# Dummy matmuls in TensorE's waits of the first batch, three first tiles beside their bank, and both q scalings of a half ahead

## The chip, the core and the metric

The kernel runs on one core of one Trainium2 chip. The core has five engines with a queue each, which run side by side and wait for each other through semaphores: TensorE (PE; its weight loads are shown as PEld), VectorE (DVE), ScalarE (ACT), GpSimd (POOL) and SyncE (SP). Each engine works through its own queue in order. The metric is the device time of one execution in microseconds; lower is better.

## What is computed

An attention layer with a cosine reweighting feeds a mixture of experts. Batch 8, 8 heads, 576 positions, head size 64; 8 experts with 512 -> 1024 -> 512.

```python
def phi(x, c, s):                       # c, s: cos and sin of a position's angle
    r = np.maximum(x, 0.0)
    return np.concatenate([r * c, r * s], axis=-1)
q_p, k_p = phi(q, cos_w, sin_w), phi(k, cos_w, sin_w)
kv = np.einsum('bhsf,bhsd->bhfd', k_p, v)
z = np.sum(k_p, axis=2)
num = np.einsum('bhsf,bhfd->bhsd', q_p, kv)
den = np.einsum('bhsf,bhf->bhs', q_p, z)[..., None] + 1e-06
x = num / den                           # heads side by side: 4608 x 512
...
P = balanced(exp(x @ w_gate))           # eight rounds over rows and columns
for e in range(E):
    out += P[:, e:e + 1] * (np.maximum(x @ w1[e], 0.0) @ w2[e])
```

## The kernel before

**Stages.** The first stage does the attention, batch after batch, and puts the first expert's two matmuls (ffn1, ffn2) between the attention's steps. The later stages balance P and run the other seven experts. The change lies in the first stage alone: in the first batch (lines 588 to 622), which has no expert work to lie between, in block j = 0, which holds the second batch's attention, and in block j = 1.

**The attention of one batch.** It goes in two halves of two head pairs (hk 0, 1 and 2, 3):
- `prep_q` scales q by cos and sin on VectorE (tile q_p). In batches 0 and 1 `turn` then transposes it on TensorE, three chunks a matmul bank, three banks a head pair, and ScalarE or VectorE takes each bank out with the relu (q_pT). From batch 2 on a transposing DMA on SP's queue does it.
- `prep_k` (relu, on ScalarE or VectorE), `prep_kp` (scaling on VectorE, tile k_p), `prep_v` (a copy into v_aug).
- `begin` is 36 small matmuls, k_p with v_aug. `made` takes the results out: zsel on VectorE, kv_sb on ScalarE.
- `denominators` is TensorE's q_pT with zsel, then VectorE's reciprocal and its split into a high and a low part (den, hi, hl).
- `attend` spreads hl over the rows (three matmuls; ScalarE copies the result to rb), multiplies q_pT with kv_sb, and VectorE multiplies both into xT, the input of the experts.

**The first expert's first tiles.** `first(kt)` adds the share of head pair kt to the first four tiles of ffn1 (two banks h_ps, two banks y_ps), each 128x512; after kt = 3 ScalarE takes them out (hT). Block 0 then begins with slot 4: slots 4 to 7 are ffn1's tiles, 8 to 15 ffn2's halves. `at(block, slot, fn, ...)` hangs a step of the attention behind a slot.

**Dummies.** `keep_busy(n)` (line 239) issues n matmuls of ones, 128x128x128, into a bank that nobody reads. Before the change there are 80 at the start and 14 ahead of the first half's sums. Their bank is one of the two of y_ps; the fourth of `first`'s tiles takes it over.

**What sets the order.** On TensorE, VectorE and ScalarE instructions are issued in the order in which the program is written (class `InOrder`, lines 101 to 118). The pools' buffers set waits on top of it: four banks small_ps, two h_ps, two y_ps, three buffers q_p, four k_p, four of each load. The loads stand in GpSimd's queue, written at lines 215 to 237 and in `load`: q, k and v of the first batch, the first expert's w1 in four parts, k, v and q of the second batch, w2 in two parts, then the batches that follow.

## Time and profile before

| | us |
|---|---|
| median of 7 runs | 996.55 |
| lowest and highest | 992.6 and 997.46 |
| the profiled execution's own time | 992.84 |
| its span, first to last instruction | 991.1 |
| TensorE busy in the span | 969.7 (98%) |
| VectorE, ScalarE, GpSimd busy | 809.1, 568.2, 59.0 |
| mean granted clock of TensorE in the span | 0.995 |

The profile is of one execution; its times count from the first instruction. A busy time is the sum of the instructions' durations on an engine. A line of the order of time has start, duration, engine, line, operation, output <- inputs, shape and count; what stands in brackets at its end is the idle time just before and the tile or DMA that ended it. Most instructions are issued through a helper and have its line, 109, so tiles tell them apart. A row of the busy table by stretches has the stretch, its length, the busy time and the count of instructions of PE, PEld, DVE, ACT and POOL, then the granted clock (1.00 is full), the busy share of the DMA engines (over 1 with overlapping packets) and GB/s.

### The profile page before, as it was taken

How to read it: one execution, taken by the hardware profiler on the slowest of the kernel's cores; microseconds unless marked ns; L12 is line 12 of the kernel's file. 1: busy time of each engine (PE TensorE's matmuls, PEld its weight loads, DVE VectorE, ACT ScalarE, POOL GpSimd, SP SyncE). 2: the span in 40 equal slices, each digit the busy share in tenths (PEclk: the TensorE clock that was granted, in tenths of full speed). 3: DMA queues.
4: the chain of work that ended last, by engine and by line, in shares of the span. 5: the costliest groups of instructions: out<-in, count | busy, mean ns of one | idle time of the engine just before them, and what ended most of it. 6: DMA issues, size and time to landing. Idle time of an engine off the chain costs nothing.

```text
span 991.1 us, 20149 instructions
## 1 busy us (share of the span) xinstructions
PE 969.7 (98%) x7804; PEld 674.7 (68%) x7804; DVE 809.1 (82%) x1840; ACT 568.2 (57%) x1267; POOL 59.0 (6%) x80
## 2 busy tenths in 40 slices
PE   7899999989999999999999999999999999999997
PEld 5445544447777777777777777777777777777775
DVE  6677675679889878988889888988789888988887
ACT  5576665457776555555555555555555555555551
POOL 6203110010000000000000000000000000000001
PEclk8999999999999999999999999999999999999999
DMA  9949991623013320043113410133103400104535
GB/s 163 207 87 155 158 151 32 133 45 90 25 49 67 62 54 25 25 92 67 34 40 67 82 34 26 41 76 67 49 25 68 91 25 25 49 25 111 132 86 128
DMA packets 80304, 73.54 MB, mean 74 GB/s; under 512 B 33232, under 2 KB 72144, under 8 KB 80208
## 3 DMA queue, kind: packets, MB, share of 16 engines
q0 software_dynamic: 27200, 30.94, 19.8%
q1 hardware_dynamic: 52768, 41.06, 16.9%
q8 instruction: 61, 1.00, 0.4%
q14 instruction: 35, 0.29, 0.1%
q10 hardware_dynamic: 240, 0.26, 0.1%
HBM read 83.12 MB, written 12.98 MB: 97 GB/s over the span
## 4 chain that ended last, share of the span: by engine, by line
PE 92%; DVE 3%; ACT 2%; DMA 1%; POOL 1%; issue 0%; POOLq 0%; ACTq 0%; SPq 0%
PE rows_ps L109 34%; PE h_ps L109 28%; PE copied_ps L109 11%; PE p_ps L109 11%; PE y_ps L109 5%; PE small_ps L109 4%; DMA v_ld<-in_v_dram 1%; ACT acc_lo L109 1%; DMA q_pT<-q_p 0%; DVE den L109 0%; DVE acc_hi L887 0%; POOL hs_last L902 0%; DVE P_tok L109 0%; DMA out_dram<-acc_lo 0%; DVE colp L109 0%
## 5 line engine op out<-in xcount | busy, mean ns | idle before, releaser
L887 DVE SCALAR_TENSOR_TENSOR acc_lo<-rows_ps,P_tok,acc_lo 128x512 f32<-128x512 f32 (+1 forms) x322 | 203.1, 639 | 74.4 <-PE rows_ps L109 74.3
L109 PEld LDWEIGHTS <-H 128*128 128x128 f16 x2080 | 203.0, 98 | 83.1 <-issue 1.2
L823 ACT CAST u<-h_ps 128x384 f16<-128x384 f32 x288 | 137.8, 478 | 131.1 <-PE h_ps L109 131.1
L109 PEld LDWEIGHTS <-w1e 128*128 128x128 f16 x1632 | 157.0, 98 | 68.4 <-issue 8.8
L817 DVE CUSTOM_DVE_ANT_0 H<-p_ps,u 128x384 f16<-128x384 f32 x329 | 180.8, 550 | 6.6 <-PE p_ps L109 6.4
L109 PEld LDWEIGHTS <-hs 128*128 128x128 f16 x1500 | 146.6, 98 | 56.2
L109 PE MATMUL h_ps<-S,w1e 128*128 128x384 f16 x672 | 164.1, 326 | 1.1 <-ACT u L109 0.9
L109 PE MATMUL p_ps<-xT,T 128*128 128x384 f16 x672 | 164.1, 326 | 0.1
L109 PE MATMUL h_ps<-xT,w1e 128*128 128x384 f16 (+1 forms) x616 | 151.5, 353 | 0.3 <-DVE xT L109 0.3
L109 PE MATMUL rows_ps<-V,H 128*128 128x256 f16 x1000 | 150.0, 273 | 0.7 <-DVE acc_hi L887 0.7
L109 PE MATMUL rows_ps<-w2e,hs 128*128 128x256 f16 x1000 | 150.0, 273 | 0.0
L855 ACT ACTIVATE H<-h_ps 128x384 f16<-128x384 f32 x144 | 70.7, 491 | 95.0 <-PE h_ps L109 95.0
L109 PEld LDWEIGHTS <-T 128*128 128x128 f16 x1008 | 98.1, 98 | 29.5 <-issue 3.1
L109 PE MATMUL rows_ps<-w2e,H 128*128 128x256 f16 (+1 forms) x568 | 91.2, 285 | 0.0
L836 ACT COPY copied_ps<-h_ps 128x384 f32<-128x384 f32 x144 | 67.5, 468 | 35.4 <-PE h_ps L109 35.4
L846 ACT ACTIVATE H<-copied_ps 128x384 f16<-128x384 f32 x144 | 70.9, 492 | 20.3 <-PE copied_ps L109 20.3
L109 PE MATMUL h_ps<-S,T 128*128 128x384 f16 x336 | 81.8, 325 | 0.4 <-ACT copied_ps L109 0.3
L109 PE MATMUL copied_ps<-xT,w1e 128*128 128x384 f16 x336 | 82.1, 326 | 0.0
L109 PE MATMUL copied_ps<-w2e,H 128*128 128x256 f16 x504 | 75.6, 272 | 0.0
L109 PE MATMUL rows_ps<-V,hs 128*128 128x256 f16 x500 | 75.0, 272 | 0.0
L887 DVE SCALAR_TENSOR_TENSOR acc_lo<-copied_ps,P_tok,acc_lo 128x256 f32<-128x256 f32 x126 | 60.0, 476 | 0.6 <-PE copied_ps L109 0.2
L887 DVE SCALAR_TENSOR_TENSOR acc_hi<-rows_ps,P_tok,acc_hi 128x512 f32<-128x512 f32 (+1 forms) x56 | 41.2, 736 | 20.5 <-PE rows_ps L109 19.7
(144 smaller groups left out, 952.2 us busy)
## 6 DMA issues: line engine op xcount, KB each, us to landing
S<-x_saved SPq DMA_DIRECT2D x108, 192.0 KB, 2.4
out_dram<-acc_lo SPq DMA_DIRECT2D x62, 128.0 KB, 2.4
w1e<-in_moe_w_dram POOLq DMA_DIRECT2D x7, 1024.0 KB, 9.1
w2e<-in_moe_w_dram POOLq DMA_DIRECT2D x7, 1024.0 KB, 10.1
q_ld<-in_q_dram POOLq DMA_DIRECT2D x16, 288.0 KB, 7.5
k_ld<-in_k_dram POOLq DMA_DIRECT2D x16, 288.0 KB, 8.6
v_ld<-in_v_dram POOLq DMA_DIRECT2D x16, 288.0 KB, 9.2
x_saved<-S SPq DMA_DIRECT2D x18, 192.0 KB, 1.9
```

The costliest lines, as they stand in the source:

```text
L109: i = getattr(self.engine, name)(*args, **kwargs)
L817: latest = ve._custom_dve(TENSOR_ADD_SAT, out=out, in0=ps[:, 0:TU], in1=t[:], s0=FP32_MAX, s1=0.0)
L823: se.copy(out=t[:], in_=ps[:, 0:TU])
L836: se.copy(out=Y[:, 0:TU], in_=X[:, 0:TU])
L846: se.activation(out=h11, in_=Y[:, 0:TU], func=AF.Relu)
L855: se.activation(out=h12, in_=X[:, 0:TU], func=AF.Relu)
L887: ve.scalar_tensor_tensor(out=a, in0=rows, scalar=P_tok[:, g, self.e : self.e + 1], in1=a, op0=ALU.mult, op1=ALU.add,)
```

## The change

The first batch's order is written anew, and dummies are put between its steps:
- `turn_all` and `attend` get a parameter `busy`: so many dummies after each turn, or between attend's two matmul groups.
- The dummies keep their bank; `first` has three tiles, and block 0 begins with slot 3. The steps that hung at slots 4 to 7 move a slot ahead or behind (begin(1, 0) is now behind slot 4), and k, v of the second batch's first half are prepared ahead of first(3).
- Both q scalings of a half are issued ahead: q of hk 2 ahead of `made`, q of hk 3 ahead of the denominators, and the turns of hk 3 ahead of attend(0, 0).
- The second v copy of each half goes to VectorE. The denominators of the second half stand ahead of first(1), first(2) between the two attends.
- In block 1 (j = 1) sums, denominators and attends hang one slot later, q of hk 2 is scaled in block 0, k of hk 1 in block 1.

```diff
--- before.py
+++ after.py
@@ -489,7 +489,7 @@
             for h in heads:
                 hls[b, h // 2] = hl
 
-        def attend(b, hk):
+        def attend(b, hk, busy=0):
 
             parts = ((0, 2 * C3), (2 * C3, C))
             rb_ps = [ps_s.tile([P, 512], FP32, name="small_ps") for _ in parts]
@@ -504,6 +504,7 @@
                         stop=True,
                     )
                 se.copy(out=rb[:, c0 * HP : c1 * HP], in_=rb_ps[i][:, 0 : (c1 - c0) * HP])
+            keep_busy(busy)
             num_ps = [ps_s.tile([P, 512], FP32, name="small_ps") for _ in parts]
             for i, (c0, c1) in enumerate(parts):
                 for hh in range(2):
@@ -560,7 +561,7 @@
                 first_ps.extend(
                     ps_h[0].tile([P, TCH], FP32, name="h_ps") if i < 2
                     else ps_y.tile([P, Dm], FP32, name="y_ps")
-                    for i in range(4)
+                    for i in range(3)
                 )
             for ft, h_ps in enumerate(first_ps):
                 te.matmul(
@@ -573,9 +574,10 @@
                 if kt == KT - 1:
                     se.activation(out=hT[:, ft, 0:TCH], in_=h_ps[:], func=AF.Relu)
 
-        def turn_all(b, hk, scalar=None):
+        def turn_all(b, hk, scalar=None, busy=0):
             for i in range(3):
                 turn(b, hk, i, scalar)
+                keep_busy(busy)
 
         begun = {}
 
@@ -587,57 +589,64 @@
 
         for hk in (0, 1):
             prep_q(0, hk)
-            turn_all(0, hk, True)
+            turn_all(0, hk, True, 4)
         for hk in (0, 1):
             prep_k(0, hk, False)
             prep_kp(0, hk)
-        keep_busy(14)
-        for hk in (0, 1):
-            prep_v(0, hk, se.copy)
+        keep_busy(8)
+        prep_v(0, 0, se.copy)
+        prep_v(0, 1, ve.tensor_copy)
         begin(0, 0)
         epsilons(0)
+        prep_q(0, 2)
         made(0, 0)
-        prep_q(0, 2)
+        prep_q(0, 3)
+        keep_busy(4)
         denominators(0, range(4))
-        turn_all(0, 2, True)
+        turn_all(0, 2, True, 4)
         prep_k(0, 2)
-        prep_q(0, 3)
-        attend(0, 0)
+        turn_all(0, 3, True, 4)
+        keep_busy(10)
+        prep_kp(0, 2)
+        attend(0, 0, 8)
         prep_k(0, 3)
+        prep_kp(0, 3)
         prep_v(0, 2, se.copy)
-        prep_kp(0, 2)
-        turn_all(0, 3)
-        prep_v(0, 3, se.copy)
-        attend(0, 1)
-        prep_kp(0, 3)
+        prep_v(0, 3, ve.tensor_copy)
+        attend(0, 1, 4)
         first(0)
         begin(0, 1)
         epsilons(0)
         made(0, 1)
+        keep_busy(4)
+        denominators(0, range(4, 8))
         first(1)
-        denominators(0, range(4, 8))
-        attend(0, 2)
-        attend(0, 3)
+        keep_busy(24)
+        attend(0, 2, 8)
         first(2)
+        attend(0, 3, 6)
+        for hk in (0, 1):
+            prep_k(1, hk, False)
+            prep_kp(1, hk)
+            prep_v(1, hk, se.copy)
         first(3)
 
         for j in range(B):
             b = j + 1
             if j == 0:
 
-                for half in range(2):
-                    for hk in (2 * half, 2 * half + 1):
-                        at(0, 4 + half, prep_k, 1, hk, False)
-                        at(0, 4 + half, prep_kp, 1, hk)
-                        at(0, 4 + half, prep_v, 1, hk, se.copy)
-                at(0, 5, begin, 1, 0)
-                at(0, 5, made, 1, 0)
-                at(0, 6, prep_q, 1, 0)
-                at(0, 6, prep_q, 1, 1)
-                at(0, 7, begin, 1, 1)
-                at(0, 7, turn_all, 1, 0)
-                at(0, 7, made, 1, 1)
-                at(0, 7, prep_q, 1, 2)
+                at(0, 4, begin, 1, 0)
+                at(0, 4, made, 1, 0)
+                for hk in (2, 3):
+                    at(0, 4, prep_k, 1, hk, False)
+                    at(0, 4, prep_kp, 1, hk)
+                    at(0, 4, prep_v, 1, hk, se.copy)
+                at(0, 5, prep_q, 1, 0)
+                at(0, 5, prep_q, 1, 1)
+                at(0, 6, begin, 1, 1)
+                at(0, 6, turn_all, 1, 0)
+                at(0, 6, made, 1, 1)
+                at(0, 6, prep_q, 1, 2)
                 at(0, 7, turn_all, 1, 1)
                 at(0, 7, prep_q, 1, 3)
                 at(0, 7, turn_all, 1, 2)
@@ -648,26 +657,27 @@
                     at(0, (10, 12, 13, 14)[hk], attend, 1, hk)
             elif b < B:
                 if j == 1:
+                    at(j, 0, prep_q, b, 3)
+                    at(j, 0, prep_kp, b, 1)
                     for hk in (2, 3):
-                        at(j, 0, prep_q, b, hk)
-                        at(j, hk - 2, prep_kp, b, hk)
-                        at(j, hk - 2, prep_v, b, hk, se.copy)
-                    at(j, 1, sums, b, 0)
-                    at(j, 3, sums, b, 1)
+                        at(j, hk - 1, prep_kp, b, hk)
+                        at(j, hk - 1, prep_v, b, hk, se.copy)
+                    at(j, 2, sums, b, 0)
+                    at(j, 4, sums, b, 1)
                 else:
                     at(j, 0, sums, b, 1)
-                at(j, 5 if j == 1 else 3, denominators, b)
+                at(j, 6 if j == 1 else 3, denominators, b)
                 for hk in range(HK):
-                    at(j, (8 if j == 1 else 6) + 2 * hk, attend, b, hk)
+                    at(j, (9 if j == 1 else 6) + 2 * hk, attend, b, hk)
             if j:
                 at(j, 5, gates, j)
             if j == 0:
                 for half in range(2):
                     at(j, 3, load, b + 1, half)
                 for slot, fn, hk, *args in (
-                    (12, prep_k, 0), (12, prep_q, 0), (13, prep_k, 1), (13, prep_kp, 0),
-                    (13, prep_v, 0, se.copy), (14, prep_q, 1), (15, prep_k, 2),
-                    (15, prep_kp, 1), (15, prep_v, 1, se.copy), (15, prep_k, 3),
+                    (12, prep_k, 0), (12, prep_q, 0), (13, prep_k, 1), (13, prep_q, 1),
+                    (14, prep_v, 0, se.copy), (14, prep_q, 2), (15, prep_k, 2),
+                    (15, prep_kp, 0), (15, prep_v, 1, se.copy), (15, prep_k, 3),
                 ):
                     at(j, slot, fn, b + 1, hk, *args)
             elif b + 1 < B:
@@ -689,7 +699,7 @@
             if j:
                 hT = hA.tile([P, FT, TCH], F16, name="hT")
             for slot in range(NS):
-                if j == 0 and slot < 4:
+                if j == 0 and slot < 3:
                     pass
                 elif slot < FT:
                     ffn1(hT, w0, j, [slot])
```

## Prediction

> **What bounds the kernel now.** I read the page's chain first, then the clock by slices, then the busy table in stretches as long as the clock's own steps, then the order of time from 10 to 42 us.

> ```profile
> PE 92%; DVE 3%; ACT 2%; DMA 1%; POOL 1%; issue 0%; POOLq 0%; ACTq 0%; SPq 0%
> ```

> TensorE (PE) carries the chain, and from 70 to 140 us each stretch of 10 us shows it 10.00 us busy. So whatever TensorE gains or loses before about 75 us arrives at the end whole. The stretch to look at is the first 75 us:

> ```profile
> PE   7899999989999999999999999999999999999997
> PEclk8999999999999999999999999999999999999999
> ...
> 4.69:8.10 3.41, 3.41 (x61) 3.31 (x59) 2.16 (x12) 1.54 (x4) 3.41 (x6) 1.00 1.05 138
> 8.10:11.51 3.41, 1.87 (x39) 1.58 (x38) 2.13 (x4) 3.10 (x8) 2.04 (x3) 1.00 1.15 185
> 11.51:14.93 3.42, 2.08 (x49) 1.27 (x44) 2.71 (x6) 1.87 (x7) 1.43 (x2) 1.00 1.27 196
> 14.93:18.34 3.41, 2.82 (x19) 1.71 (x19) 2.79 (x6) 2.93 (x7) 1.73 (x3) 0.50 1.45 196
> 18.34:21.75 3.41, 3.31 (x31) 1.37 (x31) 2.18 (x5) 0.97 (x3) 1.92 (x3) 0.50 1.27 204
> 21.75:25.17 3.42, 2.28 (x46) 1.02 (x40) 1.45 (x3) 0.43 (x2) 1.41 (x2) 1.00 1.22 208
> 25.17:28.58 3.41, 2.11 (x16) 1.14 (x17) 2.15 (x6) 1.40 (x4) 1.80 (x3) 1.00 1.22 206
> 28.58:31.99 3.41, 3.41 (x10) 1.21 (x8) 3.31 (x8) 1.72 (x4) 1.05 (x2) 0.50 1.24 206
> ```

> The column after the five engines is the granted clock. It changes only on a grid of 3.41 us, and it is 0.50 in three of these steps, 14.93 to 21.75 and 28.58 to 31.99. Each fall follows a step with little matmul work (2.08 and 2.11 us busy, much of it matmuls of 64 rows or 32 columns), each return a step full of it. Beyond 32 us it is 1.00 until the last 2 us. At half clock a 128x512 matmul starts 0.427 us after the one before it instead of 0.216. The waits that thin out those steps are VectorE's (DVE) chain from the sums to the reciprocals:

> ```profile
> 12.42 0.75 DVE L109 TENSOR_TENSOR q_p<-q_ld,acc_hi 128x1152 f16<-128x1152 f16 x1
> ...
> 13.09 1.35 DVE L109 RECIPROCAL den<-small_ps 96x192 f32<-96x192 f32 x1
> ...
> 15.37 0.66 PE L109 MATMUL small_ps<-hl,acc_hi 96*128 96x192 f16 x3 [1.47 <-DVE hl L109]
> ...
> 19.38 1.03 PE L109 MATMUL h_ps<-xT,w1e 128*128 128x512 f16 x2
> ...
> 24.07 1.35 DVE L109 RECIPROCAL den<-small_ps 96x192 f32<-96x192 f32 x1 [1.53 <-PE small_ps L109]
> ...
> 26.22 0.42 PE L109 MATMUL small_ps<-hl,acc_hi 96*128 96x192 f16 x3 [2.20 <-DVE hl L109]
> ...
> 64.16 0.34 PE L109 MATMUL small_ps<-q_pT,zsel 128*32 128x192 f16 x6 [1.40 <-DMA q_pT<-q_p]
> ```

> **The change, step by step.** Dummies: 6x4+8+4+6x4+10+8+4+4+24+8+6 = 124 against 14, at 0.056 us each (the 14 at 8.69 load weights of 0.098 within 0.82 us), 6.2 us of TensorE more. They cost nothing only where TensorE waits anyway.

> 1. To 11.1 us. 18 transposes and 32 dummies end near 10.1; the sums can't begin before 11.10, since v_ld lands only when ScalarE (ACT) starts its copy at 10.38. Cost nothing. The second v copy moves to VectorE (0.44 there at 70.38, 0.67 on ACT) and runs beside the first; the second 18 sums began at 11.68 before, now they follow at once. Gain 0.3.
> 2. First half's chain. VectorE now has a q scaling (0.67 from start to start) ahead of zsel, which waits for q_ld (landed by 12.12), and a second one ahead of the reciprocal. zsel ends near 12.9 instead of 12.51, the reciprocal starts at 13.5 instead of 13.09, hl is there at 15.7 instead of 15.32. TensorE has 18 transposes and 34 dummies to run after the denominators (52 x 0.056 = 2.9 from 13.2) and reaches attend(0, 0) at 16.1 instead of 15.37: 0.7 lost, half of it by the dummies' length. In exchange the nine transposes that stood at 16.59 (1.14 us at half clock) are done.
> 3. At full clock an attend's matmuls take 0.72 (26.22 to 26.94), two with 12 dummies (0.67) 2.1: first(0) starts at 18.2 instead of 19.38. It has three matmuls (0.65) instead of four at half clock (1.7): the second sums start near 18.9 instead of 21.20. They wait for the last v copy on VectorE, and end near 20, 2.1 earlier than before.
> 4. first(1) stood between sums and denominators (0.95, 22.55 to 23.5) and now stands behind them. Denominators start near 20.4 instead of 23.52, the reciprocal at 21.0 instead of 24.07, and 1.35 + 0.26 + 0.41 and small gaps later hl comes at 23.1 instead of 26.2: gain 3.1. first(1) and the 24 dummies (0.65 + 1.35) end at 22.8, inside that wait. Nothing is lost.
> 5. first(2) now stands between attend(0, 2) and attend(0, 3), and waits for VectorE's xT of hk 2 (1.0 us); behind it queue attend(0, 3)'s matmuls, and behind those ACT's rb copies and VectorE's last two xT. first(3) waits the same for hk 3 (1.0). ffn1's first tile then waits for the bank that ACT's relu frees (0.4). It starts at 28.6 with three tiles done, where before it started at 31.31 with four. The fourth tile costs 4 x 0.216. Gain 1.8, and 0.4 more as two matmuls at 31.3 ran at half clock.
> 6. To the first ffn2 (41.10). Batch 1's k scalings (1.0 each on VectorE) are issued ahead of first(3), so they start at once at 28 instead of 29; TensorE waits for the last k scaling for 0.5 where it waited 0.4 for ACT's v copies before. ffn2 starts near 38.5: gain 2.6. The weights and loads come in one stream (204 to 208 GB/s); everything used here lands ahead of its new time by the order in which the queue issues it, w2e last (issued at 20.74, typically 12.8 to landing), so 33.5 to 34. On GpSimd's queue only one k load and one v load of batch 3 change places (issued 32 to 38, used from about 65): nothing. That the dummies keep their bank, and first(kt) has three instead of four, costs step 5's wait for the bank and no more: before, the fourth tile took the bank after its last dummy.
> 7. Block 1 (about 54 to 76 us). ACT has the same k relus (0.70) and v copies (0.67) ahead of the relus of h_ps, and TensorE arrives earlier: it waits 1.35 for a bank where it waited 0.3 at 54.83. The denominators come one slot later and the q scalings some 4.8 earlier, so the 1.40 wait at 64.16 for the transposing DMA goes. But VectorE's queue is dense there (8.69 of 10 us from 70 to 80), and as TensorE comes earlier it waits for xT at three places, by my walk 1.1, 0.6 and 0.9; the same walk of the kernel before has 0.8 of such waits where the trace has none, so I count 1.8. Block 1: +1.4 - 1.05 - 1.8 = -1.4.

> Sum: 2.6 - 1.4 = 1.2 us earlier against the profiled execution; its own time is 992.84 (span 991.1 and 1.7 around it), so 991.6. Step 7 is the weakest: bounded by no loss at all (2.6 + 1.4 = 4.0 earlier, 988.8) and by its waits doubled (1.05 + 1.8 more, 994.5).

> **The profiled execution is no median.** It took 992.84; the seven runs have 996.55 in the middle, and reach from 992.6 to 997.46. One profile cannot show why. What it shows is a loss that depends on where the grid lies: the edges (14.93, 21.75, 28.58, 31.99) follow no instruction. Of a full step at half clock up to 1.7 us is lost (28.58 to 31.99: 3.41 us of matmuls that take 1.7), so 3.7 us are two or three more such steps. There are candidates: counted in columns (512 in 0.216 us), the two steps ahead of the falls hold about 1.3 us of matmuls, and two that stayed at 1.00 hold only 1.4 (8.10) and 1.6 (21.75). The changed kernel's poorest 3.41 us, wherever the grid lies between 8 and 36 us, holds 1.5 (around first(2)), the others 2 or more. So I take the clock as 1.00 throughout, in every run, and the median as the undisturbed walk: 991.6.

> The row: the clock fell at 14.93 with no gap of TensorE over 1.5 us before it. [...]

> **Rivals.**
> - *The runs differ for another reason* (14%). The gain against the profiled execution stays, the 3.7 us too: 996.55 - 1.2 = 995.35. For it: seven numbers and one profile prove no cause. Against: nothing else in the first 75 us idles by chance.
> - *Given back* (10%). VectorE's and ACT's queues in block 1 eat everything: 996.5, no change. For it: DVE at 8.69 of 10. Against: before, the same queue did the same work behind a 3.5 us idle (64.55).
> - *Slower: the clock still falls and each dummy doubles* (12%). If 14.93 to 21.75 and one later step stay at 0.50 in spite of the ones, some 21 matmuls left of step 2 cost 0.051 more each (1.1), the 12 dummies, two attends and first(0) of step 3 double (0.6 + 0.7 + 0.6), and a later step loses 1.7: 4.7, of which about 1 lies in waits. Against a gain of 1.2 that is 2.5 behind the profiled execution, or 999 from the median. It decides from two half-clock steps on. Against: the ones alone brought TensorE from 9 to 13 matmuls a microsecond (1 to 4 us) to 21 (5 to 6 us).

> **How the numbers follow.** Forecast (64%): 991.6, itself from 989.5 to 994. The range to leave out no more than 2 in 10 reaches over the second rival and to the third's edge: 989.5 to 996.5. About 0.2% (2 us) is what a measurement of this kernel tells from no change. Faster by more: the forecast's 64% and 4% of the first rival: 0.68. Within: 0.20. Slower by more: 0.12.

> **What would show it.** Clock 1.00 from 4.7 us to the end; hl's matmuls near 16.1 and 23.1; first ffn2 near 38.5; no wait for q_pT at 60 to 65 but waits for xT from 66 to 74; runs closer together than 992.6 to 997.46. Half-clock steps after 8 us, or ffn2 later than 40.5, would make the prediction wrong.

## The result, and the profile after

The changed kernel takes 992.35 us (median of 20 runs, 991.19 to 995.15). The kernel before takes 996.86 in the runs beside it (47 runs, 991.94 to 999.91). The ratio is 0.9962, 95% interval 0.9952 to 0.9971. The profiled execution took 992.67 (span 991.0), against 992.84 (span 991.1) before. So the two profiled executions are equal within 0.2 us, and the medians are 4.5 apart.

The page of the changed kernel, TensorE and its granted clock by slices, and the chain by engine:

```profile
PE   9899999989999999999999999999999999999997
...
PEclk9999999999999999999999999999999999999999
...
PE 92%; DVE 3%; DMA 2%; ACT 1%; issue 1%; POOL 1%; POOLq 0%; DVEq 0%; ACTq 0%; SPq 0%
```

The chain still runs on TensorE. The clock row has lost its 8 at the start. In stretches on this execution's own grid, which begins at 5.93 where that of before began at 4.69 (columns as before: span, PE, PEld, DVE, ACT, POOL, clock, DMA share, GB/s):

```profile
9.34:12.76 3.42, 2.62 (x69) 2.22 (x66) 2.85 (x6) 2.03 (x5) 1.61 (x3) 1.00 1.21 204
12.76:16.17 3.41, 3.35 (x62) 2.94 (x60) 3.34 (x8) 2.46 (x7) 1.98 (x3) 1.00 1.35 198
...
23.00:26.41 3.41, 2.40 (x32) 1.78 (x30) 1.63 (x5) 0.70 (x2) 1.63 (x3) 1.00 1.21 208
26.41:29.82 3.41, 2.25 (x20) 1.21 (x18) 1.92 (x5) 2.51 (x6) 1.54 (x3) 1.00 1.23 206
...
33.24:36.65 3.41, 2.33 (x47) 1.28 (x46) 3.34 (x7) 2.16 (x5) 1.18 (x2) 1.00 1.21 208
```

No step between 5.93 and 988.97 is at 0.50. The poorest ones hold 2.25 to 2.62 us of busy TensorE, where before two held 2.08 and 2.11 and were followed by a fall. Now the order of time, the lines that answer to those of before:

```profile
13.93 1.35 DVE L109 RECIPROCAL den<-small_ps 96x192 f32<-96x192 f32 x1
16.67 0.41 PE L109 MATMUL small_ps<-hl,acc_hi 96*128 96x192 f16 x3
19.01 0.61 PE L109 MATMUL h_ps<-xT,w1e 128*128 128x512 f16 x2
21.78 1.35 DVE L109 RECIPROCAL den<-small_ps 96x192 f32<-96x192 f32 x1 [0.89 <-PE small_ps L109]
23.93 0.42 PE L109 MATMUL small_ps<-hl,acc_hi 96*128 96x192 f16 x3
26.07 0.59 PE L109 MATMUL h_ps<-xT,w1e 128*128 128x512 f16 x2 [0.91 <-DVE xT L109]
28.74 0.59 PE L109 MATMUL h_ps<-xT,w1e 128*128 128x512 f16 x2 [0.90 <-DVE xT L109]
39.54 1.03 PE L109 MATMUL y_ps<-w2e,hT 128*128 128x512 f16 x4
```

hl's matmuls at 16.67 and 23.93 stand without a bracket: TensorE waits for nothing there, the ones fill the 1.47 and 2.20 that it waited before. It waits at first(2) and first(3) instead. The first ffn2 comes at 39.54, 1.56 earlier than before. Later, TensorE's waits from 50 to 95 us:

```profile
55.33 1.02 PE L109 MATMUL h_ps<-xT,w1e 128*128 128x512 f16 x4 [1.19 <-ACT hT L109]
68.75 0.44 PE L109 MATMUL small_ps<-q_pT,kv_sb 128*64 128x384 f16 x4 [0.65 <-DVE xT L109]
71.52 0.54 PE L109 MATMUL small_ps<-q_pT,kv_sb 128*64 128x384 f16 x4 [0.25 <-DVE xT L109]
74.94 0.95 PE L109 MATMUL small_ps<-acc_lo,k_p 64*128 64x65 f16 x36 [0.44 <-ACT rb L109]
92.79 0.54 PE L109 MATMUL small_ps<-acc_hi,kv_sb 128*64 128x384 f16 x4 [1.09 <-DVE xT L109]
```

The wait for the transposed q (1.40 at 64.16 before) is gone, and 3.6 us of waits stand there in all, against 2.2 before. The last of them, 1.09 at 92.79, has a cause of its own. In VectorE's queue that xT stands behind a q scaling of batch 4, and this one waits for a buffer that a transposing DMA still reads:

```profile
90.48 0.76 DVE L109 TENSOR_TENSOR q_p<-q_ld,acc_hi 128x1152 f16<-128x1152 f16 x1 [1.21 <-DMA q_pT<-q_p]
```

That DMA took 5.78 us from issue (84.61) to landing; the same one of before took 4.29 and made no wait. Counted by ffn2's matmuls, the changed kernel leads by 1.56 at the first, 2.74 at the 64th (73.51 against 76.25), 0.25 at the 96th (96.43 against 96.68) and 1.0 at the last matmul of the program (985.86 against 986.88); most of what it regains there is a wait of the kernel before, 0.58 at 152.72, again behind a transposing DMA (5.37). From the last matmul's start to the end of the span, with the last stores, it takes 5.1 us where it took 4.3, so that nearly all of the lead is lost again.

Where do 4.5 us of the median come from, if not from this? From the granted clock, run by run:

| kernel | runs | median us (range) | median clock (range) | median of runs at clock 0.999 or more |
|---|---|---|---|---|
| before, beside the experiments | 74 | 996.0 (991.8 to 999.3) | 0.990 (0.985 to 0.996) | none |
| changed | 20 | 992.35 (991.19 to 995.15) | 0.999 (0.997 to 1.000) | 992.25 (18) |
| e1 order alone | 12 | 991.99 (989.76 to 995.20) | 0.995 (0.989 to 1.000) | 989.76 (1) |
| e2 ones alone | 10 | 992.03 (991.02 to 993.48) | 0.998 (0.997 to 1.000) | 991.26 (5) |
| e3 half of the ones | 7 | 991.42 (988.88 to 992.20) | 0.997 (0.996 to 1.000) | 988.88 (1) |
| e4 block 1 as before | 6 | 989.12 (988.84 to 991.40) | 1.000 (0.998 to 1.000) | 988.96 (5) |
| g1 v copy back | 12 | 992.39 (991.86 to 995.05) | 0.999 (0.997 to 1.000) | 992.30 (11) |
| g2 slots back | 12 | 992.00 (989.92 to 995.92) | 0.998 (0.995 to 1.000) | 991.30 (6) |
| f1 = e4, 80 ones | 5 | 988.76 (988.34 to 990.37) | 0.999 (0.998 to 1.000) | 988.69 (4) |
| f2 = e4, no ones | 12 | 994.12 (989.96 to 996.88) | 0.992 (0.988 to 1.000) | 989.96 (1) |
| f3 = e4, ones of 32 rows | 6 | 1002.3 (999.3 to 1006.1) | 0.986 (0.982 to 0.991) | none |
| g3 = e4, ones of 32 weight columns | 10 | 992.41 (991.29 to 993.55) | 0.999 (0.999 to 1.000) | 992.41 (10) |
| g4 = e4, ones that stream 32 columns | 10 | 990.60 (989.42 to 993.72) | 0.997 (0.993 to 0.998) | none |
| f5 = f1, first(2) behind attend(0, 3) | 5 | 986.70 (986.22 to 988.08) | 1.000 (0.999 to 1.000) | 986.70 (5) |

Over the 74 runs of the kernel before, time and mean clock go together (correlation -0.90): a straight line gives 0.57 us for each 0.001, and 0.7 of scatter around it. One step of 3.41 us at half clock lowers the mean by 3.41 x 0.5 / 991 = 0.0017, so by that line it costs about 1.0, an estimate. The profiled execution of before (0.995) was one of the best (one of the 74 runs is faster); by its clock the median run (0.990) has three such steps more.

### The profile page after: what moved, and what is told of

Its sections match the earlier page's. It is cut to its first block, busy times and chain, and to the rows that moved or that the text cites. A ratio compares the mean times of both kernels' runs of the same rounds, so it can differ in the third digit from the quotient of the medians.

```text
span 991.0 us, 20371 instructions
## 1 busy us (share of the span) xinstructions
PE 971.0 (98%) x7914; PEld 680.1 (69%) x7914; DVE 809.1 (82%) x1840; ACT 567.8 (57%) x1267; POOL 59.0 (6%) x80
## 3 DMA queue, kind: packets, MB, share of 16 engines
q8 instruction: 62, 1.02, 0.4%
## 4 chain that ended last, share of the span: by engine, by line
PE 92%; DVE 3%; DMA 2%; ACT 1%; issue 1%; POOL 1%; POOLq 0%; DVEq 0%; ACTq 0%; SPq 0%
PE rows_ps L109 34%; PE h_ps L109 28%; PE copied_ps L109 11%; PE p_ps L109 11%; PE y_ps L109 4%; PE small_ps L109 4%; DMA q_ld<-in_q_dram 1%; DMA q_pT<-q_p 1%; DVE xT L109 0%; DVE den L109 0%; DVE k_p L109 0%; DVE q_p L109 0%; DVE acc_hi L897 0%; POOL hs_last L912 0%; DVE P_tok L109 0%
## 5 line engine op out<-in xcount | busy, mean ns | idle before, releaser
L109 PEld LDWEIGHTS <-H 128*128 128x128 f16 x2080 | 203.0, 98 | 83.1 <-issue 1.2
L109 PEld LDWEIGHTS <-w1e 128*128 128x128 f16 x1632 | 156.4, 98 | 69.4 <-issue 9.6
L109 PEld LDWEIGHTS <-hs 128*128 128x128 f16 x1500 | 146.6, 98 | 56.2
L109 PE MATMUL h_ps<-S,w1e 128*128 128x384 f16 x672 | 164.1, 326 | 1.1 <-ACT u L109 0.9
L109 PE MATMUL p_ps<-xT,T 128*128 128x384 f16 x672 | 164.1, 326 | 0.1
L109 PE MATMUL h_ps<-xT,w1e 128*128 128x384 f16 (+1 forms) x620 | 151.2, 351 | 3.3 <-DVE xT L109 1.8
L109 PE MATMUL rows_ps<-V,H 128*128 128x256 f16 x1000 | 150.0, 273 | 0.7 <-DVE acc_hi L897 0.7
L109 PE MATMUL rows_ps<-w2e,hs 128*128 128x256 f16 x1000 | 150.0, 273 | 0.0
L109 PEld LDWEIGHTS <-T 128*128 128x128 f16 x1008 | 98.1, 98 | 29.5 <-issue 3.1
L109 PE MATMUL rows_ps<-w2e,H 128*128 128x256 f16 (+1 forms) x568 | 91.2, 285 | 0.0
L109 PE MATMUL h_ps<-S,T 128*128 128x384 f16 x336 | 81.8, 325 | 0.4 <-ACT copied_ps L109 0.3
L109 PE MATMUL copied_ps<-xT,w1e 128*128 128x384 f16 x336 | 82.1, 326 | 0.0
L109 PE MATMUL copied_ps<-w2e,H 128*128 128x256 f16 x504 | 75.5, 272 | 0.0
L109 PE MATMUL rows_ps<-V,hs 128*128 128x256 f16 x500 | 74.9, 272 | 0.0
```

The source lines that it names most:

```text
L109: i = getattr(self.engine, name)(*args, **kwargs)
```

## The experiments

The theory (A): the ones keep the clock at 1.00 wherever its grid lies, and that is the median's gain. The rivals: R1, the new order does it, and the ones only fill; R2, the runs spread for a reason that is not the clock.

**e1, the order alone.**

```diff
 def keep_busy(n):
-    for _ in range(n):
+    for _ in range({80: 80, 14: 14}.get(n, 0)):
...
-keep_busy(8)
+keep_busy(14)
 prep_v(0, 0, se.copy)
```

> The changed kernel with its new ones matmuls taken out (the 80 at the start and the 14 behind the k preparation stay); order of the work, three first tiles and the bank set aside are as in the changed kernel. Theory A, the ones hold the clock: steps at 0.50 come back, since the stretches around hl's two waits and first(2) hold little else; but the new order has some of that work in the waits, so fewer than the kernel before: median 993.5 to 996, mean granted clock 0.995 to 0.998 in most runs, and a wide spread. Rival R1, the order of the work brings the gain and the ones only fill: 992.3 as the changed kernel, clock 0.999 or 1.000 in nearly all runs. Rival R2, the runs of the kernel before spread for another reason than the clock: times spread over 3 us or more at one and the same granted clock.

Measured: 991.99, ratio to before 0.9962 (0.9947 to 0.9977), clock from 0.989 to 1.000. The median is the changed kernel's, so R1 has that point, and A's 993.5 was wrong. But the spread is A's: 5.4 us, and the time goes with the clock (0.49 us for each 0.001, correlation -0.94). The profiled execution took 995.2; its stretches:

```profile
10.74:14.16 3.42, 1.87 (x57) 1.25 (x57) 2.01 (x6) 0.54 (x3) 1.15 (x3) 1.00 1.25 200
14.16:17.57 3.41, 3.27 (x25) 2.29 (x23) 2.82 (x5) 3.08 (x8) 2.03 (x3) 0.50 1.45 196
...
20.98:24.40 3.42, 2.09 (x47) 0.96 (x41) 2.32 (x5) 0.43 (x2) 1.80 (x3) 1.00 1.22 210
24.40:27.81 3.41, 2.47 (x10) 0.97 (x11) 0.88 (x3) 0.70 (x2) 1.69 (x3) 0.50 1.20 202
```

The same picture as before the change: a step of little matmul work, then one at 0.50. By the median clock (0.995 against 0.990) the order thins out fewer steps than the old one, and does not end it.

**e2, the ones alone,** in the order of before (main lines of the diff):

```diff
-    for i in range(4)          # first tiles
+    for i in range(3)
...
-turn_all(0, hk, True)
+turn_all(0, hk, True, 4)
...
+keep_busy(4)
 denominators(0, range(4))
-turn_all(0, 2, True)
+turn_all(0, 2, True, 4)
+keep_busy(22)
...
-attend(0, 0)
+attend(0, 0, 8)
...
 denominators(0, range(4, 8))
-attend(0, 2)
-attend(0, 3)
+keep_busy(34)
+attend(0, 2, 8)
+attend(0, 3, 6)
```

> The kernel before with ones matmuls alone: three first tiles and a bank set aside as in the changed kernel, 8 in place of 14, 4 behind each transpose of hk 0 to 3, 4 ahead of each denominators, 22 ahead of attend(0, 0), 34 ahead of attend(0, 2), and 8, 4, 8, 6 inside the four attends; every other operation stands in the order of before. Theory A: clock 0.999 to 1.000 in most runs, and the time that is left is the old order's: the chain to hl in the second half starts later, and the fourth first tile costs 0.9 of TensorE at full clock; 993 to 994.5, runs close together. Rival R1 (the order does it): 996.5 or more, with steps at 0.50 as in the kernel before.

Measured: 992.03, ratio 0.9963 (0.9951 to 0.9975), better than A's figure, and clock 0.997 or more in all ten runs (0.999 or more in five, where A expected most). So the order alone gives 992.0, the ones alone give 992.0, and both together 992.35: they do not add up. Something in the changed order gives back what a better clock brings.

**e3, half of the ones.** `range(n if n == 80 else n // 2)` in keep_busy.

> The changed kernel with half of its 124 ones matmuls at every place (the 80 at the start stay). It asks how much margin the clock has. Theory A with a threshold of the work in one step: the poorest stretches lose 0.2 to 0.7 us of matmuls, most still hold over 1.8 of 3.41; 992 to 993, a step at 0.50 in up to a third of the runs. If the clock asks for nearly all of them: 993.5 or more with 0.997 or less in most runs. R1: 992.3 with clock 1.00 in all.

Measured: 991.42, clock 0.996 to 0.998 in six of seven runs. Fewer steps were safe than expected (a third was expected to lose one, most do), and the time is no worse: at the same clock the kernel with fewer ones is the faster one (its one run at 1.000 took 988.88).

**e4, batch 2's work where it was.**

```diff
-at(j, 0, prep_q, b, 3)
-at(j, 0, prep_kp, b, 1)
 for hk in (2, 3):
-    at(j, hk - 1, prep_kp, b, hk)
-    at(j, hk - 1, prep_v, b, hk, se.copy)
-at(j, 2, sums, b, 0)
-at(j, 4, sums, b, 1)
+    at(j, 0, prep_q, b, hk)
+    at(j, hk - 2, prep_kp, b, hk)
+    at(j, hk - 2, prep_v, b, hk, se.copy)
+at(j, 1, sums, b, 0)
+at(j, 3, sums, b, 1)
...
-at(j, 6 if j == 1 else 3, denominators, b)
+at(j, 5 if j == 1 else 3, denominators, b)
...
-    at(j, (9 if j == 1 else 6) + 2 * hk, attend, b, hk)
+    at(j, (8 if j == 1 else 6) + 2 * hk, attend, b, hk)
...
-(12, prep_k, 0), (12, prep_q, 0), (13, prep_k, 1), (13, prep_q, 1),
-(14, prep_v, 0, se.copy), (14, prep_q, 2), (15, prep_k, 2),
-(15, prep_kp, 0), (15, prep_v, 1, se.copy), (15, prep_k, 3),
+(12, prep_k, 0), (12, prep_q, 0), (13, prep_k, 1), (13, prep_kp, 0),
+(13, prep_v, 0, se.copy), (14, prep_q, 1), (15, prep_k, 2),
+(15, prep_kp, 1), (15, prep_v, 1, se.copy), (15, prep_k, 3),
```

> The changed kernel with batch 2's work at the end of block 0 and in block 1 (q scalings, k and v preparation, sums, denominators, attends) in the slots of the kernel before; the first batch and its ones are as changed. By step 7 of the prediction the undoing brings the wait for the transposed q back (1.4 lost) and takes the waits for xT away (1.8 won): 992.0. If the move costs because it puts batch 2's attends one slot later, next to block 2's first matmul (a wait for xT of 1.09 us at 92.79 in the changed kernel's trace): that wait goes too and the transposed q is in time, 991.0 to 991.5. If the move is needed because TensorE arrives earlier at batch 2's transposes: 993.5 or more.

Measured: 989.12, ratio 0.9941 (0.9924 to 0.9957), below all that was expected. At clock 0.999 or more it is 988.96 against 992.25 of the changed kernel: with all 124 ones in place, undoing the move of batch 2's work is worth 3.3. All waits of TensorE from 50 to 95 us in its profile:

```profile
52.47 1.24 PE L109 MATMUL h_ps<-xT,w1e 128*128 128x512 f16 x5 [0.26 <-DVE xT L109]
57.52 0.46 PE L109 MATMUL small_ps<-acc_lo,k_p 64*128 64x65 f16 x18 [0.51 <-DVE k_p L109]
89.88 0.54 PE L109 MATMUL small_ps<-acc_hi,kv_sb 128*64 128x384 f16 x4 [0.59 <-DVE xT L109]
```

1.4 in place of 3.6. In block 1, where the move is, it is 0.8 in place of 2.5; the rest is the 0.59 in block 2. The wait for the transposed q, which was to come back, does not stand there: its fourth transposing DMA lands 3.4 after its issue, where the one of before took 4.9.

The 3.3 is not the price of the move alone. The two profiles are 3.7 apart: 0.8 of it is there at the first ffn2 (38.75 against 39.54), before any of the moved work, 2.1 comes from there to the 96th, and 0.8 behind the last matmul. And with the move left in, the only runs of e3 and e1 at clock 1.000 took 988.88 and 989.76, as little as those without it (988.96 in e4, 989.96 in f2, which has e4's order and no ones). So it looks as if the move and the full number of ones are dear only together; these are single runs at full clock, and why it should be so, no run tells.

**g1 and g2, which half of that move.** g1 puts `(14, prep_v, 0, se.copy)` back to slot 13 in the changed kernel; g2 puts back the five lines of block 1 for sums, denominators and attends, and leaves the end of block 0 as changed.

> The changed kernel with one move of the last part of block 0 undone: batch 2's first v copy on ScalarE in slot 13 again in place of 14. The undoing of all of batch 2's moves (e4_block1_old) took 2.8 off at clock 1.00; this asks how much of it is ScalarE's queue ahead of block 1's relus (a wait of 1.2 for the bank at 55.33 in the changed kernel's trace, 0.3 in e4's). If the v copy alone is that wait: about 1 earlier than the changed kernel, 991.3. If not: 992.3.

> The changed kernel with the other move undone: batch 2's sums in slots 1 and 3, its denominators in slot 5 and its attends in slots 8, 10, 12, 14 of block 1 again, the end of block 0 as changed. If the waits of the attends for xT (0.9, and 0.4 to 0.8 at two more places) come from that later slot: 0.9 to 1.7 earlier than the changed kernel, 990.7 to 991.4; if TensorE only waits elsewhere for the same queue: 992.3.

g1: 992.39; its profile still waits 0.82 for the bank at 55.37. The v copy is not the cause. g2: 991.30 at full clock, 0.95 earlier, as expected, but half of its runs are at 0.998 or less. A wait in its profile, and the stretches around it, show a place where a step falls:

```profile
59.00 0.46 PE L109 MATMUL small_ps<-acc_lo,k_p 64*128 64x65 f16 x18 [1.23 <-DVE k_p L109]
```

```profile
56.22:59.63 3.41, 1.77 (x42) 0.90 (x40) 3.35 (x6) 3.01 (x7) 0.00 (x0) 1.00 0.94 174
59.63:63.04 3.41, 3.41 (x21) 1.20 (x21) 1.06 (x3) 1.67 (x5) 0.00 (x0) 0.50 0.45 84
```

With the sums in their old slot and the k scaling of hk 1 still in its new one, the sums wait for k_p, that thins out a step, and the clock falls in a place that has no ones. In this profile the two halves belong together; what each of them is worth by itself stays open.

**f1 and f2, the ones on e4's order.** f1 keeps 80 of 124 (2 in place of 4 behind the transposes of hk 2 and 3; 0, 4, 0 in place of 10, 8, 4 around attend(0, 0) and attend(0, 1); 16, 4, 4 in place of 24, 8, 6 in the second half). f2 has none, by e1's edit.

> The kernel of the run e4_block1_old (batch 2's work in the slots of before) with 80 of the 124 ones matmuls: 2 in place of 4 behind each transpose of hk 2 and 3, none in place of 10 and 4 in place of 8 at attend(0, 0), none in attend(0, 1), 16 in place of 24 and 4 in place of 8 at attend(0, 2), 4 in place of 6 in attend(0, 3). If 44 fewer at 0.056 us only leave waits longer and the clock has margin: 989.0 as e4, or up to 0.4 earlier, where the ones stood on the path to hl (step 2 of the prediction puts half of 0.7 on their length); clock 1.00. If the clock needs them, as the halved ones hint (0.997 in most runs): 990 to 991.5.

> The kernel of e4_block1_old without the new ones matmuls (80 and 14 stay). The runs of the order alone gave 0.49 us for each 0.001 of mean granted clock, and 990.0 at clock 1.00. Theory A: median clock 0.995 again, so 2.5 above what e4 has at clock 1.00 (989.2) less the 0.5 or so that the ones themselves cost: 991, spread from 988.5 to 994. If the order alone now keeps TensorE busy enough: 988.7 in nearly all runs at 1.00.

f1: 988.76, as e4: between 80 and 124 ones no difference shows (0.3 at full clock). Its runs fall into two groups, 988.3 to 988.8 and 990.2 to 990.4, and the profiled one (990.16, clock 0.999) shows a cause of spread that is not the clock, a late load:

```profile
13.80 0.76 DVE L109 TENSOR_TENSOR q_p<-q_ld,acc_hi 128x1152 f16<-128x1152 f16 x1 [2.04 <-DMA q_ld<-in_q_dram]
14.75 0.56 PE L109 MATMUL small_ps<-q_pT,zsel 128*32 128x192 f16 x12 [1.43 <-DVE zsel L109]
```

The new order scales q of hk 2 ahead of zsel, so that the chain to the reciprocal begins with the landing of this load, and TensorE waits 1.43 for it.

f2: 994.12, with a clock between 0.988 and 1.000 and 0.48 us for each 0.001. This is the plainest answer to R1: the same order with ones takes 988.8 to 989.1, without them 994.1. That it is 2.1 slower than e1 is mostly its clock (0.992 against 0.995 in the median, 1.4 by its own line). Up to 45 us both issue the same work, so the grid and the loads are the candidates for which steps fall there: in the profiles of e1, e3 and g2 TensorE waits 1.4, 1.0 and 1.7 us for zsel, which stands behind the scaling of q of hk 2, and 0.4 in f2's; in e1's the wait ends at 13.54, in the step ahead of the first fall.

**f3, g3 and g4, ones of another shape.** All three are e4 with another shape of the 124 ones (the 80 at the start stay):

```diff
-out=idle_ps[:, 0:P], lhsT=ones_sq[:], rhs=ones_sq[:]
+out=idle_ps[:, 0:P], lhsT=ones_sq[0:32], rhs=ones_sq[0:32]         # f3, thin
+out=idle_ps[0:32, 0:P], lhsT=ones_sq[:, 0:32], rhs=ones_sq[:]      # g3, narrow
+out=idle_ps[:, 0:32], lhsT=ones_sq[:], rhs=ones_sq[:, 0:32]        # g4, short
```

> The kernel of e4_block1_old with ones matmuls of 32 rows in place of 128 behind the first 80: as many instructions, 128 columns each as before, so the same time of streaming, but a quarter of the array's rows. If the clock goes by the time in which columns stream: 989.1 and clock 1.00 as e4. If it goes by how much of the array works: like no ones, 991 with a median clock near 0.995 and a wide spread.

> e4_block1_old with the new ones matmuls 32 weight columns wide (32 rows of output) in place of 128, all 128 rows fed. Thin ones (32 rows fed) let the clock fall at 11.36 after a step in which TensorE was busy for 3.36 of 3.41 us. If what counts is the product of rows and columns of the array that work: half-clock steps as with thin ones, 996 to 1002. If only the rows that are fed count: 989.1 with clock 1.00.

> e4_block1_old with new ones matmuls that stream 32 columns in place of 128, through the whole array. If the clock counts what the array does in a step, a quarter of the streaming counts a quarter, and the ones end sooner: half-clock steps in many runs as without ones, 990.5 to 994. If it counts instructions or loads of weights: 989.0 with clock 1.00.

f3: 1002.3, ratio 1.0074 (1.0049 to 1.0100): slower than without any ones, and than before. Its stretches:

```profile
7.95:11.36 3.41, 3.36 (x43) 2.34 (x42) 2.01 (x5) 2.88 (x7) 1.89 (x4) 1.00 1.18 188
11.36:14.77 3.41, 3.09 (x58) 1.98 (x57) 2.10 (x6) 0.70 (x3) 1.74 (x3) 0.50 1.28 201
14.77:18.19 3.42, 3.42 (x28) 1.96 (x24) 2.02 (x3) 1.84 (x4) 1.63 (x3) 0.50 1.45 196
```

TensorE is busy for 3.36 of 3.41 us, and the clock falls all the same. It stays at 0.50 for five steps, to 28.43, and each thin one takes 0.107 instead of 0.056. That is what the prediction's third rival describes. With narrow ones, in the same place:

```profile
10.39:13.80 3.41, 3.04 (x71) 2.31 (x68) 1.57 (x5) 2.08 (x5) 1.78 (x3) 1.00 1.21 200
13.80:17.22 3.42, 3.42 (x53) 2.23 (x47) 2.87 (x6) 2.42 (x7) 1.77 (x3) 1.00 1.44 196
```

less is busy, and the clock stays: 0.999 or 1.000 in all ten runs, where f3's six have 0.982 to 0.991. So in these runs ones of 32 rows did not hold the clock, and ones of 128 rows did, with 32 weight columns as with 128 (0.998 to 1.000 in e4). g3 is slower for another reason, told at the end. g4, with short ones, is in between: 990.60, with a clock of 0.993 to 0.998, so that by the estimate above a step or more is lost in every run. In its profile TensorE is busy for 1.93 of 3.41 us in the step at 9.33, where e4 has 2.94 in the one at 8.56, and the next step is at 0.50.

**f5, first(2) behind attend(0, 3) again,** on f1:

```diff
 attend(0, 2, 4)
-first(2)
 attend(0, 3, 4)
+first(2)
```

> f1_fewer_ones with first(2) behind attend(0, 3) again, as in the kernel before, so that attend(0, 3)'s matmuls no longer queue behind first(2)'s wait for VectorE's xT (1.0 in the traces of the changed kernel and e4, start to start 1.15 against 0.22), and ScalarE's rb copies and VectorE's last two xT no longer behind those. By step 5 of the prediction this wait is a loss that the changed order makes: 1 to 1.4 earlier than f1, 987.5 to 988. Rival: TensorE then waits as long for hk 3's xT at first(3) or for the k scalings of batch 1: as f1, 989.

Measured: 986.70, ratio to before 0.9917 (0.9902 to 0.9932); 2.1 earlier than f1, more than expected, and the fastest kernel of the study, 5.6 below the changed kernel's median. f1's first(2) and first(3), then f5's:

```profile
27.03 0.59 PE L109 MATMUL h_ps<-xT,w1e 128*128 128x512 f16 x2 [0.90 <-DVE xT L109]
...
29.59 0.59 PE L109 MATMUL h_ps<-xT,w1e 128*128 128x512 f16 x2 [0.90 <-DVE xT L109]
```

```profile
25.33 0.60 PE L109 MATMUL h_ps<-xT,w1e 128*128 128x512 f16 x2
...
26.27 0.59 PE L109 MATMUL h_ps<-xT,w1e 128*128 128x512 f16 x2
```

Both waits are gone, and none comes in their place: from hl's matmuls to ffn1's first tile it takes 4.06 (23.27 to 27.33) instead of 5.53 (25.11 to 30.64). That is 1.5 of the 2.1; f1's late load in some runs is a candidate for the rest.

## Why the prediction was right, point by point

It forecast 991.6, and 992.35 was measured. The point that decides, the clock, was right. The walk beneath it was right in most terms; the 1.2 that it promised in the profiled execution shrank to 0.2, and one term in it was over-counted.

- **The profiled execution is no median:** right. The 3.7 us were put down to two or three more half-clock steps; the table's line gives 2.9 more steps (0.995 to 0.990) at about 1.0 each. "1.00 in every run" was nearly so: 18 of 20 runs at 0.999 or more, and the two at 0.997 are the slowest (994.68 and 995.15). These two are 2.4 and 2.9 behind the median of the others, more than the 1.7 that one step can lose by the prediction's estimate, so something else falls together with the step there; no such run was profiled. Columns alone, by which the prediction weighed the steps, do not part them: f3's step at 7.95 holds 43 matmuls of 128 columns and was followed by 0.50, e1's at 7.33 holds 28 and was not. One reading was off: the clock of before is 1.00 to its last instruction, not until 2 us before it. What the ones are worth by the clock, f2 against e4 shows: 5.0, and against f1, of the same round of runs, 5.4.
- **Step 1:** the transposes and ones were done by 10.8 instead of 10.1, since the clock rose at 5.93 instead of 4.69 and the 80 ones before them ended 0.6 later. But that set nothing: TensorE then waited 0.80 for ScalarE's v copy, since v landed at 10.89 (10.36 before) and k at 9.40 (8.42). The second 18 sums did follow the first at once. The sums began at 11.64 instead of 11.10.
- **Step 2:** the reciprocal at 13.93 (13.5 expected), hl's matmuls at 16.67 (16.1): 0.5 later, otherwise as walked, and with no wait. The chain begins with the landing of q, as the step says, but q landed later than in the profile of before (12.30 against 11.83). The changed kernel's line, then e4's, which has the same work up to there:

```profile
12.33 0.76 DVE L109 TENSOR_TENSOR q_p<-q_ld,acc_hi 128x1152 f16<-128x1152 f16 x1 [0.42 <-DMA q_ld<-in_q_dram]
```

```profile
11.54 0.76 DVE L109 TENSOR_TENSOR q_p<-q_ld,acc_hi 128x1152 f16<-128x1152 f16 x1 [0.51 <-DMA q_ld<-in_q_dram]
```

- **Step 3:** first(0) at 19.01 (18.2), 0.4 earlier than before instead of 1.2, for the same reason.
- **Step 4:** the reciprocal at 21.78 (21.0), hl's matmuls at 23.93 (23.1). first(1) and the 24 ones fit into the wait, as expected.
- **Step 5:** first(2) waits 0.91, first(3) 0.90, ffn1's first tile 0.25: as walked. f5 shows that this price was not needed.
- **Step 6:** first ffn2 at 39.54 instead of 38.5, a gain of 1.56 instead of 2.6. Most of the missing 1.0 is the late landing of q: in e4 it comes 0.79 earlier, and the reciprocal (13.14), hl's matmuls (15.88), first(0) (18.22) and the first ffn2 (38.75) all come 0.79 earlier too. The clock's late rise does not set it, since TensorE had waited 0.80 when the sums began. The prediction's terms add up to 2.2 (1.8 and 0.4 of step 5); where the rest of the 2.6 comes from it does not say.
- **Step 7:** the terms came as sized, with one more behind them. The wait for the transposed q went (1.4), the bank costs 0.9 more (1.05 expected), the waits in the attends and at the sums behind them are 1.3 (1.8 expected). The wait of 1.09 at 92.79, in block 2, was not foreseen; it is not the move's, since f3, g3 and g4, without the move, have it too (1.5, 1.2, 1.5). What was over-counted is the first term: "The denominators come one slot later and the q scalings some 4.8 earlier, so the 1.40 wait [...] goes". With the move, TensorE waits for no transposing DMA between 4 and 140 us, in the changed kernel's profile and in e3's. But that is worth 1.4 only against an execution in which this DMA takes 4.9, as in the profile of before. In the changed kernel's profile it took 3.5, and in e4, which undoes the move, 3.4, without a wait. In these executions the move had nothing to gain on this term.

Of the rivals, "the runs differ for another reason" falls with the correlation of -0.90 and with f2 and f3, which change the ones alone; the loads explain part of the scatter around the line. "Given back" was half true, at 10%: in the profile, blocks 1 and 2 give back 1.3 of the 1.56, and the median's gain is the clock's. That 991.6 came so near is partly luck. The walk lacked, on one side, a load that landed 0.5 later, the wait of 1.09 in block 2 and 0.8 at the end of the span, and on the other two waits of before that went (0.51 for k_p at 59.87, 0.58 at 152.72); only together do they leave the forecast 0.8 off. At equal clock the changed kernel is not faster than before: 992.25 against 990.5, where the line of before ends at clock 1.00 (drawn on from 0.996, so an estimate). "The clock still falls and each dummy doubles" did not come: the clock is 0.997 to 1.000 in the 20 runs. f3, whose ones feed 32 rows, shows what it costs when it falls (1002.3).

Left open: the 124 ones and the move together cost what the ones' clock brings on this order (991.99 without the ones, 992.35 with them), though each is cheap without the other (e1 and e4, by few runs at full clock). The waits in block 1 explain 1.8 of the 3.3 between the changed kernel and e4, and one profile of each does not show whether the rest comes in every run.

## What to carry to other kernels

## What the runs showed of the hardware

**Busy time does not part the steps.** Nine falls of the clock came behind steps in which TensorE was busy for 1.77 us (g2 at 56.22), 1.87 (e1 at 10.74), 1.93 (g4 at 9.33), 2.04 (f2 at 9.80 and 20.04), 2.08 and 2.11 (before at 11.51 and 25.17), 2.09 (e1 at 20.98) and 3.36 (f3 at 7.95), of 3.41 each. After 1.87 (before at 8.10, e1 at 7.33), 2.25 (the changed kernel at 26.41, e4 at 25.63), 2.33 and 2.40 (the changed kernel at 33.24 and 23.00) and 3.04 (g3 at 10.39) the clock stayed at 1.00. f3 and g3 differ in the shape of the ones alone: 32 rows into 128 weight columns in f3, 128 rows into 32 weight columns in g3. What besides busy time decides, these runs do not show.

**The grid lay elsewhere in each profile.** In the profile of before the clock rises at 4.69, in the changed kernel's at 5.93, though both start with the same 80 ones at 1.14: up to the rise the ones start 0.107 us apart, from there on 0.056. In both every later edge lies a whole number of 3.41 us behind the rise. The experiments' steps as counted here begin anywhere from 3.92 (e1) to 6.98 (g3). The grid moves the end of the 80 ones (the 80th starts at 7.24 in before, at 7.83 in the changed kernel), but the 0.79 between e4 and the changed kernel, with the same work up to the first ffn2, come from a load: the q that the reciprocal's chain begins with, for which VectorE waits until 11.54 in e4, 12.33 in the changed kernel and 13.80 in f1.

**Groups of mixed tile shapes took longer.** Three transposes (128x128) and four ones take 0.39 us from start to start in e4 (7.51 to 7.90). With thin or narrow ones, as many columns, they take 0.60 at full clock (f3 from 7.81 to 8.40, g3 from 8.97 to 9.57): 0.1 for each change between a full and a partial tile, an estimate. g3 is 3.4 slower than e4 at the same clock; twelve such groups make 2.5 of it, an estimate. In the two profiles 2.9 is there at the first of hl's matmuls (18.80 against 15.88), 0.9 of which comes from the later end of the 80 ones (the transposes begin at 8.38 in g3, at 7.51 in e4).

**Some transposing DMAs take longer.** Of the 24 in each profile, 19 in before and 18 in the changed kernel's take 3.18 to 3.70 us to land, the others up to 5.37 and 5.78. Batch 2's fourth one took 4.9 to 5.0 in before, e2 and f2, where TensorE waits 1.4 to 1.5 for it, and 3.3 to 3.4 in e4, f1, f3 and f5, which have f2's order around it. Batch 4's first one took 5.78 in the changed kernel's profile, where VectorE waits 1.21 for it and TensorE then 1.09 for xT, and 4.29 in before, where nothing waits. Why, no run tells.
